# Order of transposes, logits and first loads in a fused attention and expert kernel

## The chip, the cores and the metric

The kernel runs on one core of a Trainium2 chip. The metric is device microseconds of one execution. Before the change the median of three runs is 722.9 us (722.79 to 723.34).

The core's engines are named in the profile as PE (TensorE, matrix products and transposes; PEld is its loading of weights), DVE (VectorE), ACT (ScalarE), POOL (GpSimd) and SP (SyncE, which only issues transfers). Products land in PSUM, eight banks of 512 float32 for each of 128 partitions; another engine has to copy them out.

## The reference

Attention in a sliding window, then a layer of experts of which each token uses one. Everything is float32.

```python
# q, k, v: (8 batches, 8 heads, 576 tokens, 64)
scores = scale * np.matmul(q, k.transpose(0, 1, 3, 2))
mask = (rel >= 0) & (rel < 64)              # a token sees itself and 63 before it
scores = np.where(mask, scores, -1e9)
attn = softmax(scores)
out = np.matmul(attn, v)
x = out.transpose(0, 2, 1, 3).reshape(4608, 512)
logits = x @ w_gate                          # (4608, 8)
expert_idx = np.argmax(logits, axis=1)
gate_w = softmax(logits)[token, expert_idx]
for e in range(8):                           # w1: (8, 512, 1024), w2: (8, 1024, 512)
    h = np.maximum(x[of e] @ w1[e], 0.0)
    y[of e] = h @ w2[e]
return gate_w[:, None] * y
```

## The kernel before, in words

**Two stages.** The attention stage runs from 0 to about 215 us and writes x, already multiplied by its gate, to a table in DRAM (`x_dram`). The expert stage gathers x by expert in tiles of 256 tokens, multiplies it by w1 and w2 (in a form with seven products instead of eight, which is where `left_sums` and `right_sums` belong) and scatters the rows to the output. The order of instructions on every engine is the order in which the code emits them (`manual_schedule`); each engine works through its own list and waits where an operand or a buffer is not ready.

**Units and steps.** The batches are taken two at a time (`bg`, four groups of batches) and the heads two at a time (`g`, four pairs): 16 units. The 1152 tokens of a unit are nine blocks of 128 and are worked on in three steps of three blocks (`ST` = 3, `NST` = 3): `N` = 48 steps in all. A unit's q and k come as eight transfers of 128 KB (`load_qk`), its v as four (`load_v`). The last 64 tokens of every batch, the rests, are loaded once for a group of batches (`load_rests`: two transfers each for q, k and v). GpSimd copies v into a second tile, shifted by a window.

`step(s)` (line 940) is a pipeline by hand, which works on several steps' data at once:

- `scored(s + 1)`: the scores of the next step on TensorE, into banks 0 and 1 (line 627); `masked` (VectorE, line 640) and `softened` (six exps on ScalarE, line 650) follow at once in those engines' lists.
- `weighted(s - 1)`: probabilities times values, into bank 6 (line 673); `divided(s - 1)` on VectorE divides by the sum and writes x (line 687).
- `logit(s - 3)`: the logits of one step, three products into bank 7 (line 710), which gathers them over the four pairs of heads.
- `flipped(s)`: six transposes of the probabilities, one bank for each head (line 658); VectorE copies the first bank out, ScalarE the second (line 660).
- `turned(s + 3)`: the transposes of q and of k for a later step (line 594, four each, one bank each, copied by ScalarE, line 599), or in a unit's third step two transposes of the rests (line 586) in one bank. A step with q and k is called long here and a step with the rests short.
- `x_turned(s - 2)`: three transposes of x (line 698), copied by ScalarE (line 701).
- then the operations that were put down for this step (`todo`).

**The ring of banks.** All these transposes take their banks from one ring of four, `tr_ring` (banks 2 to 5), in the order in which they are emitted. A transposed group can start when the copy that empties the bank's last content is done.

**Routing.** When a group of batches has its logits (`ripe`), `by_tokens` copies them to SBUF and transposes them, one step's worth after the other, and `choose` finds the expert, the gate and the rank of each token, cut into parts that are put down for later steps by `after`. `place` (VectorE) prepares the tables of tokens, `weigh` (GpSimd, some on ScalarE) multiplies x by its gate, `store` sends x to `x_dram`. For the third group of batches `after` ends with `first_tiles` in step 45: two operations of VectorE, 54 small products (line 913), one operation of VectorE that makes the table `perm_e`, and `gather_first`, which gathers the first tile of the expert stage from `x_dram` on GpSimd (line 284). The gather waits for the stores of x.

**The end of the stage.** After step 47 the code emits by hand: the last `weighted`, `turn()` (transposes of the gathered rows, line 305), the last logits and transposes of x among the first products of expert 0 (`tile0`, line 343), and the routing of the last group of batches. The first products use banks 0, 1 and 6.

**The start.** SP issues, in this order: unit 0's q and k, the gate's weights, a row of zeros for `x_dram`, the rests, unit 0's v, unit 1's q and k, unit 1's v, unit 2's q and k. ScalarE's queue carries four transfers of w1 in steps 1, 2, 4 and 5.

Of the kernel before, what the change touches and what calls it, by code (L numbers as in the profile page):

```python
# [11 lines left out]
F32 = mybir.dt.float32  # L12
# [24 lines left out]
def kernel(  # L37
# [10 lines left out]
    nc = tc.nc  # L48
    P = nc.NUM_PARTITIONS
    B, H, S, D = q.shape  # L50
    NT, DM = out.shape
    E = moe_w_gate.shape[1]
# [3 lines left out]
    NG = H // 2  # L56
# [28 lines left out]
    ident = consts.tile([P, P], F32, name="ident")  # L85
# [409 lines left out]
    with tc.manual_schedule(), ExitStack() as held, ExitStack() as brief:  # L495
# [2 lines left out]
        rp = held.enter_context(tc.tile_pool(name="rp", bufs=2))  # L498
        att = brief.enter_context(tc.tile_pool(name="att", bufs=2))
        xp = brief.enter_context(tc.tile_pool(name="xp", bufs=3))  # L500
        sc_ring, tr_ring = cycle((0, 1)), cycle((2, 3, 4, 5))


# [32 lines left out]
        def load_qk(u):  # L536
            bg, g = units[u]
            qks[u] = [qk_m(((u % 3 + 2) % 3 * 2 + n) * 1024, BG, NV, 2, D) for n in range(2)]
            for i in range(BG):
                for t, src in zip(qks[u], (q, k)):  # L540
                    for h in range(2):
                        nc.sync.dma_start(
                            out=t[:, i, :, h, :],
                            in_=src[bg * BG + i, 2 * g + h, 0:SM, :].rearrange("(p j) d -> p j d", j=NV),
                        )

        def load_rests(bg):

            at = 6144 + bg % 2 * 2048
            vr = qk_m(at + 1024, BG, H, D)  # L550
            rests[bg] = [qk_m(at, H, D), qk_m(at + 512, H, D), vr]
            for t, src in zip(rests[bg], (q, k)):
                for i in range(BG):
                    nc.sync.dma_start(
                        out=t[i * D : (i + 1) * D], in_=src[bg * BG + i, :, SM:S, :].rearrange("h p d -> p h d")
                    )
            for i in range(BG):
                nc.sync.dma_start(out=vr[D:P, i], in_=v[bg * BG + i, :, SM:S, :].rearrange("h p d -> p h d"))
# [105 lines left out]
        def weighted(s, pTs):  # L664
            u, c = divmod(s, NST)
            bg, g = units[u]
            va, vb = v_ring[u % NVR]
            px = banks[6](0, 2, ST, VW)
            for m in range(ST):
                for a, (bp, i) in enumerate(blocks_of(c * ST + m)):  # L670
                    vt = va[:, bp, i // 2] if i % 2 or i == 0 else vb[:, bp, i // 2 - 1]
                    for h in range(2):
                        nc.tensor.matmul(  # L673
                            px[a * D : (a + 1) * D, h, m, :], lhsT=pTs[h][:, m, a * D : (a + 1) * D],
                            rhs=vt[:, h, :], start=True, stop=True, skip_group_check=True,
                        )
            return px
# [35 lines left out]
                )  # L713
            return g == NG - 1

        def by_tokens(bg, c):

            if c == 0:
                logits_of[bg] = rp.tile([P, NTB, E], F32, name="logits")
            lgT = rp.tile([ST * GE, P], F32, name="lgT")  # L720
            nc.scalar.copy(out=lgT[:], in_=lgs[bg][:, c, :])
            yield
            tr = banks[next(tr_ring)](0, ST, P)
            nc.tensor.transpose(out=tr[:, 0, 0 : ST * GE], in_=lgT[:], identity=ident[0 : ST * GE, 0 : ST * GE])
            V.tensor_copy(
                out=logits_of[bg][:, c * ST : (c + 1) * ST, :],
                in_=tr[:, 0, 0 : ST * GE].rearrange("p (m e) -> p m e", e=GE)[:, :, 0:E],
            )

        last = B // BG - 1  # L730
# [146 lines left out]
        def after(s, routing, bg):  # L877
# [16 lines left out]
            for m in range(NTB):  # L894
                do(3 + m // 3, partial(place, bg * NTB + m))
                do((2, 2, 3, 3, 4, 4, 4, 5, 5)[m], partial(weigh, bg, m, nc.scalar if m in (2, 6) else G))
                if m % ST == ST - 1:
                    do(3 + m // ST, partial(store, bg, m // ST, G))
            do(6, first_tiles)

        def first_tiles():

# [4 lines left out]
                out=hi_e[:], in0=_inner(key[:], NE * C), in1=_ins(hi_id[:, C + 1 : C + 1 + NE * C], 1, NJE),  # L907
                op=ALU.is_equal,
            )
            slots = banks[next(tr_ring)](0, NE * C)  # L910
            for j in range(NJE):
                for i in range(2):
# [2 lines left out]
                    )  # L915
            V.tensor_scalar(out=perm_e[:], in0=slots, scalar1=-1.0, scalar2=float(NT), op0=ALU.mult, op1=ALU.add)
            gather_first(perm_e[:, 0:C])

        N = NU * NST
        load_qk(0)  # L920
        nc.sync.dma_start(out=wg[:, :, 0:E], in_=moe_w_gate.rearrange("(g p) e -> p g e", p=P))
        nc.sync.dma_start(out=x_dram[NT : NT + 1, :], in_=zrow[:])
        load_rests(0)
        load_v(0)
        load_qk(1)
        load_v(1)
        load_qk(2)

        for g in range(NG):
            step = NST * (g // 2) + g % 2 + 1  # L930
# [9 lines left out]
        def step(s):  # L940
            if 0 <= s + 1 < N:
                prs[s + 1] = softened(*masked(s + 1, scored(s + 1)))
            if 0 <= s - 1 < N:
                px = weighted(s - 1, pTs.pop(s - 1))
            ripe = 0 <= s - 3 < N and logit(s - 3)
            if 0 <= s < N:
                pTs[s] = flipped(prs.pop(s))
            if 0 <= s - 1 < N:
# [8 lines left out]
                    load_qk(u + 3)  # L957
            if s + 3 < N:
                turned(s + 3)
            if 0 <= s - 2 < N:  # L960
                x_turned(s - 2)
            for op in todo.pop(s, ()):
                op()
            if ripe:
                bg, c = (s - 3) // (NG * NST), (s - 3) % NST
                parts = by_tokens(bg, c)
                next(parts)
                todo.setdefault(s + 1, []).append(partial(next, parts, None))
                if c == NST - 1:
                    after(s + 1, choose(bg), bg)  # L970


        for n, s in enumerate((N - 6, N - 3)):
# [174 lines left out]
```

## Time and profile before

| what | value |
|---|---|
| median of the runs | 722.9 us (722.79 to 723.34) |
| the profiled execution | 721.0 us, span 719.3 us, mean granted TensorE clock 0.986 |
| busy over the span | PE 687.2, PEld 606.0, DVE 495.5, ACT 258.6, POOL 350.3 us |
| 0 to 28.2 us (first loads, first steps) | PE 18.8, DVE 10.0, ACT 14.2, POOL 12.6 us busy; clock 0.94 |
| 28.2 to 178.3 us (steps 3 to 40) | PE 149.3, DVE 126.3, ACT 129.9, POOL 84.1 of 150.1 us busy; clock 1.00 |
| 178.3 to 215.5 us (steps 41 to 47 and the first transposes behind) | PE 30.7, DVE 27.2, ACT 22.6, POOL 25.8 of 37.2 us busy; clock 0.91 |
| 215.5 to 719.3 us (experts) | PE 488.5 of 503.8 us busy; clock 0.99 |
| a long step, a short step | 4.07 and 3.42 us from scores to scores |

A line of the timeline gives the start, the length, the engine, the line of the kernel, the operation, out<-in with shapes, the number of instructions merged, and in brackets how long the engine was idle before and what ended that. A product of float32 counts as two instructions of PE, a transpose as one. An idle time matters where the engine is the one that the next work waits for. The granted clock is the share of TensorE's full clock.

### The profile page before, as it was taken

How to read it: one execution, taken by the hardware profiler on the slowest of the kernel's cores; microseconds unless marked ns; L12 is line 12 of the kernel's file. 1: busy time of each engine (PE TensorE's matmuls, PEld its weight loads, DVE VectorE, ACT ScalarE, POOL GpSimd, SP SyncE). 2: the span in 40 equal slices, each digit the busy share in tenths (PEclk: the TensorE clock that was granted, in tenths of full speed). 3: DMA queues.
4: the chain of work that ended last, by engine and by line, in shares of the span. 5: the costliest groups of instructions: out<-in, count | busy, mean ns of one | idle time of the engine just before them, and what ended most of it. 6: DMA issues, size and time to landing. Idle time of an engine off the chain costs nothing. (4 is left out here: it accounts for less than half of the span.)

```text
span 719.3 us, 17940 instructions
## 1 busy us (share of the span) xinstructions
PE 687.2 (96%) x6882; PEld 606.0 (84%) x6882; DVE 495.5 (69%) x1636; ACT 258.6 (36%) x653; POOL 350.3 (49%) x360
## 2 busy tenths in 40 slices
PE   5999999999879999999999999999999999999992
PEld 3788888888769897897999999999899799889992
DVE  3576898898956768676676677568666668756731
ACT  4788888888745012101221111112111122111110
POOL 4223648469573108767451545645266745262001
PEclk9999999999989999999999999999999999999997
DMA  8997789879433364517102620630441810211000
GB/s 158 220 212 176 167 195 236 205 177 248 166 106 117 117 221 171 172 59 282 46 16 84 215 84 31 230 125 15 151 169 59 282 59 6 63 31 61 15 18 29
DMA packets 137293, 93.41 MB, mean 130 GB/s; under 512 B 117008, under 2 KB 117008, under 8 KB 137170
## 3 DMA queue, kind: packets, MB, share of 16 engines
q1 hardware_dynamic: 127858, 62.16, 32.2%
q0 software_dynamic: 8736, 27.53, 11.7%
q10 hardware_dynamic: 576, 2.10, 1.0%
q8 instruction: 74, 1.21, 0.7%
q14 instruction: 49, 0.40, 0.2%
HBM read 72.89 MB, written 20.45 MB: 130 GB/s over the span
## 5 line engine op out<-in xcount | busy, mean ns | idle before, releaser
L314 DVE STREAM_TRANSPOSE v_m<-qk_m 32x256 f32<-32x256 f32 x304 | 132.3, 435 | 9.1 <-DMA qk_m<-x_dram,at_g 2.9
L343 PE MATMUL bank<-qk_m,s 128*128 128x128 f32 x1024 | 122.5, 275 | 0.7 <-DVE qk_m L364 0.7
L343 PEld LDWEIGHTS bank<-qk_m,s 128*128 128x128 f32 x1024 | 118.3, 192 | 0.9 <-issue 0.9
L274 POOL DMA_INDIRECT qk_m<-x_dram,at_g x38 | 41.0, 1079 | 141.5 <-DVE v_m L314 113.1
L650 ACT ACTIVATE pr<-pr,mx 128x128 f32<-128x128 f32 x288 | 89.7, 390 | 33.0 <-DVE mx L640 32.7
L343 PE MATMUL bank<-qk_m,w 128*128 128x128 f32 x768 | 93.9, 275 | 0.6 <-PEq L1076 0.6
L343 PEld LDWEIGHTS bank<-qk_m,w 128*128 128x128 f32 x768 | 90.6, 192 | 4.1 <-issue 3.7
L294 POOL DMA_INDIRECT out_dram<-v_m,at_s x42 | 42.4, 1010 | 87.7 <-DVE v_m L383 85.6
L640 DVE CUSTOM_DVE_ANT_0 pr<-bank,mask 128x128 f32<-128x128 f32 x288 | 64.4, 286 | 27.6 <-PE bank L627 26.3
L383 DVE TENSOR_TENSOR v_m<-bank,v_m 128x256 f32<-128x256 f32 (+1 forms) x95 | 43.8, 480 | 44.7 <-PE bank L387 30.1
L568 POOL COPY v_m<-v_m 64x520 f32<-64x520 f32 x32 | 19.8, 620 | 68.8 <-DMA v_m<-in_v_dram 66.1
L139 POOL TENSOR_TENSOR s<-w 128x1024 f32<-128x1024 f32 x22 | 52.2, 2374 | 0.0
L673 PEld LDWEIGHTS bank<-v_m,pT 128*64 128x64 f32 x1152 | 41.1, 140 | 11.4 <-DVE xs L687 5.2
L673 PE MATMUL bank<-v_m,pT 128*64 128x65 f32 x1152 | 47.8, 231 | 2.5 <-DVE xs L687 2.5
L350 ACT COPY qk_m<-bank 128x512 f32<-128x512 f32 x16 | 9.4, 587 | 108.3 <-PE bank L343 70.0
L387 PE MATMUL bank<-qkT_m,v_m 128*128 128x256 f32 x216 | 48.3, 379 | 0.0
L627 PE MATMUL bank<-qkT_m 64*64 64x128 f32 x1152 | 45.6, 290 | 0.1
L387 PEld LDWEIGHTS bank<-qkT_m,v_m 128*128 128x128 f32 x216 | 41.0, 190 | 5.5
L443 PEld LDWEIGHTS bank<-qk_m,w 128*128 128x128 f32 x320 | 43.9, 190 | 0.9 <-issue 0.7
L443 PE MATMUL bank<-qk_m,w 128*128 128x160 f32 x320 | 44.4, 299 | 0.4 <-ACT qk_m L326 0.4
L594 PE MATMUL bank<-ident,qk_m 128*128 128x128 f32 x256 | 35.7, 283 | 7.7 <-DMA qk_m<-in_q_dram 7.0
L658 PE MATMUL bank<-ident,pr 128*128 128x128 f32 x288 | 43.0, 287 | 0.0
(174 smaller groups left out, 1226.9 us busy)
## 6 DMA issues: line engine op xcount, KB each, us to landing
w<-in_moe_w_dram SPq DMA_DIRECT2D x11, 2048.0 KB, 9.5
qk_m<-in_q_dram SPq DMA_DIRECT2D x72, 128.0 KB, 3.4
qk_m<-in_k_dram SPq DMA_DIRECT2D x72, 128.0 KB, 3.5
v_m<-in_v_dram SPq DMA_DIRECT2D x64, 128.0 KB, 3.9
qk_m<-in_moe_w_dram SPq DMA_DIRECT2D x3, 2048.0 KB, 10.9
x_dram<-xs POOLq DMA_DIRECT2D x6, 512.0 KB, 4.2
x_dram<-xs POOLq DMA_DIRECT2D x3, 768.0 KB, 5.2
w<-in_moe_w_dram ACTq DMA_DIRECT2D x4, 512.0 KB, 4.5
```

The lines of the kernel that those rows point to most:

```text
L139: op()
L294: put = G.indirect_dma_start(out=out[:, :], out_offset=bass.IndirectOffsetOnAxis(ap=at_s[:, c : c + 1], axis=0), in_=ys[c], in_offset=None ...
L314: V.transpose(out=xn[b * QD : (b + 1) * QD, :, :, a * QD : (a + 1) * QD].rearrange("p c g i -> p (c g) i"), in_=rows[a * QD : (a + 1) * QD ...
L343: nc.tensor.matmul(acc[:, f, :], lhsT=a[:, g, f * P : (f + 1) * P], rhs=b[:, g, :], start=(first and f == 0 and g == 0), stop=(g == HG - 1 ...
L383: plus = lambda out, a, b: V.tensor_tensor(out=out, in0=a, in1=b, op=ALU.add)
L387: nc.tensor.matmul(acc, lhsT=a[:, f, :], rhs=b[:, f, :], start=(start and f == 0), stop=(stop and f == HF - 1), skip_group_check=True,)
L443: nc.tensor.matmul(acc[:, i], lhsT=w1[:, g, f * P : (f + 1) * P], rhs=xq[:, g].rearrange("p c s -> p (c s)")[:, 0:HALF], start=(i + g == 0 ...
L627: nc.tensor.matmul(out_, lhsT=qT[rows, t, a * WINDOW : (a + 1) * WINDOW], rhs=rhs, start=True, stop=True, skip_group_check=True,)
L640: V.tensor_tensor_reduce(out=prs[h][:, m, :], in0=scs[h][:, m, :], in1=mask[:, m0 + m, :], scale=-scale, scalar=-2 * MASKED, op0=ALU.add, ...
L650: nc.scalar.activation(out=y, in_=y, func=AF.Exp, scale=-1.0, bias=mx[:, h, m : m + 1])
L658: nc.tensor.transpose(out=tr[:, m, :], in_=prs[h][:, m, :], identity=ident[:])
L673: nc.tensor.matmul(px[a * D : (a + 1) * D, h, m, :], lhsT=pTs[h][:, m, a * D : (a + 1) * D], rhs=vt[:, h, :], start=True, stop=True, skip_ ...
```

## The change

- **x first.** `x_turned(s - 2)` is emitted ahead of `flipped(s)`, where it was behind `turned(s + 3)`. The order of the ring in a step was two of the probabilities, q, k, x; it becomes x, two of the probabilities, q, k.
- **Logits by unit.** The logits of a unit's three steps are emitted together, in the unit's third step, and `by_tokens` takes all three steps of a group of batches at once: one copy, three transposes into one bank, one copy. The end of the stage still uses one step's worth at a time.
- **First table a step later.** `first_tiles` is cut in two: its first VectorE operations stay in step 45, the products, the table and the gather move to step 46.
- **Last values in score banks.** The values of steps 46 and 47 go to banks 0 and 1 instead of 6.
- **First loads.** k of unit 0 and the rests' k of the first batches are issued on ScalarE's queue. On SP the order is unit 0's q, the rests, unit 1's q and k, v of units 0 and 1, the gate's weights, unit 2's q and k, the row of zeros.

```diff
+        lt = brief.enter_context(tc.tile_pool(name="lt", bufs=1))
         sc_ring, tr_ring = cycle((0, 1)), cycle((2, 3, 4, 5))
@@ load_qk
-                for t, src in zip(qks[u], (q, k)):
+                for t, src, queue in zip(qks[u], (q, k), (nc.sync, nc.sync if u else nc.scalar)):
                     for h in range(2):
-                        nc.sync.dma_start(
+                        queue.dma_start(
@@ load_rests
-            for t, src in zip(rests[bg], (q, k)):
+            for t, src, queue in zip(rests[bg], (q, k), (nc.sync, nc.sync if bg else nc.scalar)):
                 for i in range(BG):
-                    nc.sync.dma_start(
+                    queue.dma_start(
@@ weighted
-            px = banks[6](0, 2, ST, VW)
+            px = banks[6 if s < N - 2 else s - N + 2](0, 2, ST, VW)
@@ by_tokens
-        def by_tokens(bg, c):
+        def by_tokens(bg, c, n=1):
...
-            lgT = rp.tile([ST * GE, P], F32, name="lgT")
-            nc.scalar.copy(out=lgT[:], in_=lgs[bg][:, c, :])
+            lgT = (rp if n == 1 else lt).tile([ST * GE, n, P], F32, name=f"lgT{n}")
+            nc.scalar.copy(out=lgT[:], in_=lgs[bg][:, c : c + n, :])
             yield
-            tr = banks[next(tr_ring)](0, ST, P)
-            nc.tensor.transpose(out=tr[:, 0, 0 : ST * GE], in_=lgT[:], identity=ident[0 : ST * GE, 0 : ST * GE])
+            tr = banks[next(tr_ring)](0, n, ST * GE)
+            for i in range(n):
+                nc.tensor.transpose(out=tr[:, i], in_=lgT[:, i], identity=ident[0 : ST * GE, 0 : ST * GE])
             V.tensor_copy(
-                out=logits_of[bg][:, c * ST : (c + 1) * ST, :],
-                in_=tr[:, 0, 0 : ST * GE].rearrange("p (m e) -> p m e", e=GE)[:, :, 0:E],
+                out=logits_of[bg][:, c * ST : (c + n) * ST, :],
+                in_=tr.rearrange("p n me -> p (n me)").rearrange("p (m e) -> p m e", e=GE)[:, :, 0:E],
             )
@@ after
-            do(6, first_tiles)
+            table = first_tiles()
+            do(6, partial(next, table))
+            do(7, partial(next, table))
@@ first_tiles
+            yield
             slots = banks[next(tr_ring)](0, NE * C)
...
             gather_first(perm_e[:, 0:C])
+            yield
@@ first loads
         load_qk(0)
+        load_rests(0)
+        load_qk(1)
+        load_v(0)
+        load_v(1)
         nc.sync.dma_start(out=wg[:, :, 0:E], in_=moe_w_gate.rearrange("(g p) e -> p g e", p=P))
+        load_qk(2)
         nc.sync.dma_start(out=x_dram[NT : NT + 1, :], in_=zrow[:])
-        load_rests(0)
-        load_v(0)
-        load_qk(1)
-        load_v(1)
-        load_qk(2)
@@ step
-            ripe = 0 <= s - 3 < N and logit(s - 3)
+            ripe = 0 <= s - 3 < N and s % NST == NST - 1 and [logit(n) for n in range(s - 5, s - 2)][-1]
+            if 0 <= s - 2 < N:
+                x_turned(s - 2)
             if 0 <= s < N:
                 pTs[s] = flipped(prs.pop(s))
...
             if s + 3 < N:
                 turned(s + 3)
-            if 0 <= s - 2 < N:
-                x_turned(s - 2)
             for op in todo.pop(s, ()):
                 op()
             if ripe:
-                bg, c = (s - 3) // (NG * NST), (s - 3) % NST
-                parts = by_tokens(bg, c)
+                bg = (s - 3) // (NG * NST)
+                parts = by_tokens(bg, 0, NST)
                 next(parts)
                 todo.setdefault(s + 1, []).append(partial(next, parts, None))
-                if c == NST - 1:
-                    after(s + 1, choose(bg), bg)
+                after(s + 1, choose(bg), bg)
```

## The prediction

> **What bounds the kernel now.** I read the page's busy shares first, then windows by stage, then the timeline of one step of the attention stage, then who waits for whom, last the timelines of the head and of the end of that stage. Page, with the clock row:
>
> ```profile
> PE 687.2 (96%) x6882; PEld 606.0 (84%) x6882; DVE 495.5 (69%) x1636; ACT 258.6 (36%) x653; POOL 350.3 (49%) x360
> ...
> PEclk9999999999989999999999999999999999999997
> ```
>
> TensorE is the bound, but the change touches only 0 to 215 us, where the windows show TensorE idle 9.4 us before 28.2, 0.8 in 28.2 to 178.3 (ScalarE 130 and VectorE 126 busy of 150) and 6.5 in 178.3 to 215.5. So there is something to win at both ends, and in the middle only by less matmul work. One long step (four transposes each of q and k), timeline of TensorE; columns are start, length, engine, line:
>
> ```profile
> 102.49 0.89 PE L627 MATMUL bank<-qkT_m 64*64 64x128 f32 x24
> 103.31 0.97 PE L673 MATMUL bank<-v_m,pT 128*64 128x65 f32 x24
> 104.21 0.42 PE L710 MATMUL bank<-xT,wg 128*32 128x128 f32 x6
> 104.56 0.88 PE L658 MATMUL bank<-ident,pr 128*128 128x128 f32 x6
> 105.27 1.04 PE L594 MATMUL bank<-ident,qk_m 128*128 128x128 f32 x8
> 106.14 0.49 PE L698 MATMUL bank<-ident,xs 128*128 128x128 f32 x3
> 106.56 0.89 PE L627 MATMUL bank<-qkT_m 64*64 64x128 f32 x24
> ```
>
> From start to start: scores 0.82, values 0.90, logits 0.35, probabilities' transposes 0.71, q and k 0.87 (0.109 each), x 0.42: 4.07. A short step (rests, two transposes) takes 3.42. The same step on VectorE and ScalarE:
>
> ```profile
> 103.54 0.29 DVE L640 CUSTOM_DVE_ANT_0 pr<-bank,mask 128x128 f32<-128x128 f32 x1 [0.21 <-PE bank L627]
> ...
> 103.87 1.86 ACT L650 ACTIVATE pr<-pr,mx 128x128 f32<-128x128 f32 x6
> ...
> 105.64 0.46 ACT L660 COPY pT<-bank 128x384 f32<-128x384 f32 x1
> ```
>
> Masking begins when the scores are done; the exps begin E after the scores' start (here 1.38) and take 1.77 up to ScalarE's next instruction.
>
> The transposes' banks are a ring of four, so a group waits for the evacuation of the group four places earlier. Before, x is fifth and waits for the step's first probability copy; it shows where VectorE is late:
>
> ```profile
> 186.38 0.55 DVE L660 COPY pT<-bank 128x384 f32<-128x384 f32 x1
> ...
> 186.99 0.55 PE L698 MATMUL bank<-ident,xs 128*128 128x128 f32 x3 [1.42 <-DVE pT L660]
> ```
>
> The copy ends 186.93, TensorE goes on 0.06 later; all such waits are 4.3 us.
>
> **Steps 3 to 40, x moved ahead.** Order of banks now: q, k, after x: x, p0, p1, q, k. k, not x, is now the fifth, and k takes the bank of the same step's x. ScalarE evacuates that x behind the next step's six exps, which it was given first. So k can start at E + 1.77 + 0.48 (x copy, L701) + 0.06, and the next scores start 4 x 0.109 + 0.09 later (x itself: 0.42 = 3 x 0.109 + 0.09): a long step is E + 2.84, with E = 1.38 it is 4.22, although TensorE's work without the logits would be 4.07 - 0.35 = 3.72. The logits taken out of long steps thus go into a wait. The E of the 26 long steps 3, 4, 6, 7, ... 39, 40, read from the timeline, sum to 43.1 and their lengths to 108.5: new lengths 43.1 + 26 x 2.84 = 116.9, +8.4. Where E is above 1.4 (1.8 to 2.7 at steps 16, 21, 24, 28, 31, 33, 40) VectorE is late, from routing and from the place instructions; before, that lateness is hidden behind the rest of the step; after, it is on the path. If the longer steps let VectorE catch up wholly, E is about 1.36 and the sum is +0.7. I take +8.0, near the read E: the step after a lengthened one is less late, but one after a short step is later, because the batched logits there push the first probability copy back by about 0.7 where the step grows by 0.4.
>
> **Logits by unit.** One group of three goes from 0.35 in every step to nine in the short step. A lone group's 0.35 is six passes in three column groups side by side and a drain; two more groups add passes only. Weight loads of 0.025 (0.15 for six) give +0.30; two passes of 0.109 per group give +0.44; two full groups would be +0.70. I take +0.40, nearest the passes, for 13 short steps (5 to 41): +5.2 (3.9 to 9.1). The tokens' transposes (L724) cost 0.09 + 0.14 + 0.09 to 0.15 per group of batches before and three in a row after: nothing, hidden or not. Their copies become one on ScalarE (0.26 x 3 to about 0.48) and one on VectorE (0.18 x 3 to about 0.25); two places, off TensorE's path except through E: within 0.3 for the three groups of batches. The new pool of one buffer is rewritten once in 12 steps; no wait. Each of the three buffers of x is rewritten right behind the batch that read it, which TensorE has passed by the time the copy comes up: nothing.
>
> **The head.** SP issues one 128 KB piece per 0.66 us; TensorE waits for pieces until 20 us:
>
> ```profile
> 18.52 0.63 PE L594 MATMUL bank<-ident,qk_m 128*128 128x128 f32 x4 [1.80 <-DMA qk_m<-in_q_dram]
> ...
> 21.83 1.62 PE L673 MATMUL bank<-v_m,pT 128*64 128x65 f32 x24
> ...
> 25.12 0.89 PE L627 MATMUL bank<-qkT_m 64*64 64x128 f32 x24
> ```
>
> Six pieces (k and its rests) go to ScalarE's queue: 6 x 0.66 = 4.0 us on ScalarE before its table load (1.28, at 0.81 before), together about 6.1, against its first copy at 5.97: 0.1 late. The gate and the zero row move behind: 1.0 us less ahead. Unit 2, ahead of the zero row and behind everything else, is needed at step 3. v moves behind unit 1, so values(0) waits for 24 pieces, 3.15 MB, and behind it on TensorE stand the flips of step 1 and unit 1's second half. Data flows from 2.25 us; at 215 GB/s (busy slices 200 to 220) that is 14.6, 1.15 to land (the first pair, 4.82 less 2.25 less 1.4), and GpSimd's three copies 1.4: 19.4, where values(0) started at 21.83: -2.4. Scores, flips and unit 1 all come earlier than that, TensorE is then waiting for v, and it is warm or not: 21.83 to 25.12 took 3.29, at full clock 0.90 + 0.71 + 0.87 = 2.5. Between -2.4 and -3.2 I take -3.0; bounds 0 (two queues get in each other's way by 2.4) and -4.2 (230 GB/s, warm). By the rows issue was the limit, by little: 0.66 a piece against 0.61 at 215 GB/s. [...] If nothing but the new order counted, values(0) would come at 24 x 0.66 + 3.5 + 1.4 = 20.7, and the head would give -1.1 instead of -3.0.
>
> **The end of the stage.** Before, the table's matmuls stand in TensorE's order before the last scores and wait for VectorE:
>
> ```profile
> 202.01 1.58 PE L913 MATMUL bank<-hi_e,lo 128*128 128x4 bf16 x54 [2.69 <-DVE hi_e L906]
> ...
> 203.52 1.55 PE L627 MATMUL bank<-qkT_m 64*64 64x128 f32 x24
> ...
> 206.12 1.12 POOL L284 DMA_INDIRECT qk_m<-x_dram,perm_e  x1 [3.11 <-DVE mx L640]
> ...
> 209.56 0.97 PE L673 MATMUL bank<-v_m,pT 128*64 128x65 f32 x24 [0.88 <-DVE xs L687]
> ...
> 212.90 0.97 PE L673 MATMUL bank<-v_m,pT 128*64 128x65 f32 x24 [0.88 <-DVE xs L687]
> 213.79 1.09 PE L305 MATMUL bank<-ident,qk_m 128*128 128x128 f32 x8
> ```
>
> After the 2.69 the granted clock is 0.50 over 202 to 207 (scores 1.55 instead of 0.89). A step later the matmuls find their operand (hi_e) ready, and the score banks remove the two waits of 0.88 (the products that use banks 0 and 1 next come after both divisions, and before they waited on bank 6 no less): 2.69 + 2.5 + 1.76 = 7.0 at most. But the first gather at 206.12, with its memset and the second pair moved along on GpSimd, where nothing stands between, is not held by the table (ready 203.9): the last stores of x, issued until 202.5, take about 3.6 to land. GpSimd's chain of weighing sets those, and it starts with ScalarE's weighing in step 42, which moves with E there (3.75). The second gather starts at 208.06 and lands 3.4 later, at 211.5; after, with ScalarE 0.4 later in step 42 and the table ready about 206.8 (exps of step 45 to 202.5, 1 later than before; x and p1 copies to 203.3; values, x and flips 2.0; table 1.3; VectorE 0.2), at about 212.5. Turning gathered rows ends then at 213.0 instead of 214.8. So -1.8, whatever steps 42 to 47 gain or lose; bounds -3.3 (nothing late) and +1.7 (TensorE idle before the gather, and clock 0.5 for one stretch of 3.4 us). Later work keeps its order and is shifted.
>
> **Sum.** -3.0 + 8.0 + 5.2 - 1.8 = +8.4 on the profiled execution's 721.0 (span 719.3): 729.4. The median of the runs, 722.9, stands 1.9 above: 731.3, I say 731.
>
> **Rivals.**
> - *VectorE catches up*: +0.7 in the long steps: 722.9 + 0.7 + 5.2 - 4.8 = 724. For it: VectorE is idle 24 of 150 us; against: its lateness returns in every group of batches.
> - *k isn't held* (the other side): if k's start did not wait for x's copy, long steps become 3.72: 26 of them 96.7 instead of 108.5, or -11.8; total -11.8 + 5.2 - 4.8 = -11.4: 711.5. It decides from a mean long step of 4.16 (26 x 0.016 = 0.4, what the rest leaves): the mean before is 4.17. Against it: the wait at 186.99 shows the ring; for it only that no row shows k itself waiting.
> - *Ends pay nothing*: v lands late (0), clock falls before the gather (+1.7): 722.9 + 13.2 + 1.7 = 738.
>
> **How the numbers follow.** Main case 0.60, 726 to 736 on its own; VectorE catches up 0.18 (721 to 726); k not held 0.09; ends pay nothing 0.13. Leaving out the third case and the top of the last: 720.5 to 738. A measurement can tell about 0.2% (1.4 us): faster 0.09 + 0.05 of the second case, same 0.06, slower 0.80.
>
> **What would show it.** Right: k's transposes idle about 0.5 us in long steps behind ScalarE's x copy, long steps 4.2 or more, short 3.8; values(0) at 19 to 20; no wait at the table, the gather's landing before the turn instead. Wrong: long steps at 3.7; q and k in one run without a gap; logits' nine taking 1.05; a halved clock in the steps.

## The result

The changed kernel takes 735.6 us (median of 4 runs, 735.32 to 738.44) where the kernel before takes 723.1 us on the same chip: a ratio of 1.0171, 95% interval 1.0148 to 1.0194. It is slower by 12.5 us; +8.4 and 731 were forecast. Times are medians over the executions; one execution of the kernel with only the end changed took 1402 us and is not in its ratio. The profiled execution took 735.83 us with a span of 734.1 us, against 721.0 and 719.3 before, which is 14.8 us of span.

The page of the changed kernel first, its busy times and its clock row:

```profile
PE 689.5 (94%) x6882; PEld 608.9 (83%) x6882; DVE 492.6 (67%) x1630; ACT 259.6 (35%) x647; POOL 351.3 (48%) x360
...
PEclk9999999999999999999999999999999999999997
```

TensorE has as many instructions as before and 2.3 us more busy time (689.5 against 687.2), while the span grew by 14.8. So the loss is idle time of TensorE and not work. The page's list of the costliest groups says which idle time (after the second bar: idle time just before the group, and the releaser that ended most of it):

```profile
L595 PE MATMUL bank<-ident,qk_m 128*128 128x128 f32 x256 | 41.6, 292 | 21.6 <-ACT xT L702 14.3
```

L595 holds the transposes of q and k of the long steps. TensorE stands before them for 14.3 us because of one ScalarE copy, that of the transposed x. The timeline of two steps of the changed kernel shows the mechanism (start, length, engine, line, operation, wait in brackets; VectorE's rows are left out):

```profile
105.50 0.82 PE L659 MATMUL bank<-ident,pr 128*128 128x128 f32 x6
...
105.76 1.86 ACT L651 ACTIVATE pr<-pr,mx 128x128 f32<-128x128 f32 x6 [1.98 <-DVE mx L641]
...
106.16 0.60 PE L595 MATMUL bank<-ident,qk_m 128*128 128x128 f32 x4
...
107.53 0.45 ACT L702 COPY xT<-bank 128x384 f32<-128x384 f32 x1
107.89 0.47 ACT L661 COPY pT<-bank 128x384 f32<-128x384 f32 x1
108.04 0.66 PE L595 MATMUL bank<-ident,qk_m 128*128 128x128 f32 x4 [1.28 <-ACT xT L702]
108.63 0.89 PE L628 MATMUL bank<-qkT_m 64*64 64x128 f32 x24
...
112.29 0.66 PE L595 MATMUL bank<-ident,qk_m 128*128 128x128 f32 x4 [0.31 <-ACT xT L702]
```

The transposes of x (L699) start at 105.12 and end by 105.67 (the flips, the transposes of the probabilities, follow at 105.50), but the copy that empties their bank stands in ScalarE's order behind the six exponentials of the next step, and starts at 107.53. q's four transposes run at 106.16, k's four need the bank of x and wait 1.28 us. Four and a quarter microseconds on, the next long step shows the same wait, 0.31 us there because its exponentials were not late.

Stretch by stretch, from the starts of the steps in the two timelines (step s begins with scores(s+1)), and against the prediction's terms:

| stretch | predicted | profiled execution |
|---|---|---|
| up to the start of step 3 | -3.0 | -1.9 |
| 26 long steps, 3 to 40 | +8.0 | +10.4 |
| 13 short steps, 5 to 41 | +5.2 | +5.2 |
| step 42 to the first product of expert 0 | -1.8 | +0.4 |
| after it | 0 | +0.7 |
| sum | +8.4 | +14.8 |

The medians are 12.5 apart and not 14.8, since the median before (723.1) stands 2.1 us above its profiled execution and the median after 0.2 below its own. The table compares one execution with one: executions of one kernel differ by more than a microsecond (the kernel before took 720.6 to 728.2 over 31 of them), so its small terms are uncertain by about as much.

The head of the changed kernel, first the issues of SyncE, then TensorE, then two windows (the stretch, its length, busy times of TensorE, its weight loads, VectorE, ScalarE and GpSimd, granted clock, DMA share, GB/s):

```profile
0.82 2.98 SPq L543 DMA_DIRECT2D qk_m<-in_q_dram  x4
4.22 2.77 SPq L555 DMA_DIRECT2D qk_m<-in_q_dram  x2
...
19.70 0.46 PE L674 MATMUL bank<-v_m,pT 128*64 128x65 f32 x8
20.90 0.73 PE L674 MATMUL bank<-v_m,pT 128*64 128x65 f32 x16 [0.74 <-POOL v_m L573]
...
23.24 0.89 PE L628 MATMUL bank<-qkT_m 64*64 64x128 f32 x24
...
6.00:14.00 8.00, 6.38 (x44) 4.87 (x44) 1.17 (x11) 4.46 (x8) 2.00 (x6) 1.00 1.40 175
14.00:20.00 6.00, 6.00 (x70) 4.94 (x68) 2.08 (x16) 4.57 (x14) 0.34 (x1) 1.00 1.31 217
```

SyncE's pieces of 128 KB follow each other every 0.75 us (2.98 for four) and then every 1.39 (2.77 for two), where it was 0.66 before. An issue itself still takes 0.6 to 0.85 us; the 2.77 for two holds 1.5 us in which SyncE stood, by the profile, until an earlier piece of q had landed. The transfers moved 175 GB/s from 6 to 14 us, with the DMA engines' share at 1.40, and 217 only from 14 to 20. The first values still start at 19.70, 2.1 us earlier than before, but their second part waits for v, and scores(3), with which step 2 begins, come at 23.24, 1.9 us earlier.

The end of the stage, TensorE and GpSimd of the changed kernel:

```profile
201.82 0.66 PE L595 MATMUL bank<-ident,qk_m 128*128 128x128 f32 x4 [2.68 <-ACT xT L702]
...
203.25 1.62 PE L674 MATMUL bank<-v_m,pT 128*64 128x65 f32 x24
...
219.25 1.50 PE L918 MATMUL bank<-hi_e,lo 128*128 128x4 bf16 x54
221.87 1.12 POOL L284 DMA_INDIRECT qk_m<-x_dram,perm_e  x1 [4.61 <-DVE perm_e L921]
...
225.43 0.66 PE L305 MATMUL bank<-ident,qk_m 128*128 128x128 f32 x4 [0.32 <-DMA qk_m<-x_dram,perm_e]
227.31 1.11 PE L305 MATMUL bank<-ident,qk_m 128*128 128x128 f32 x4 [1.22 <-DMA qk_m<-x_dram,perm_e]
229.63 2.34 PE L343 MATMUL bank<-qk_m,w 128*128 128x128 f32 x16
```

The wait of 2.69 us at the table is gone: L918 waits for nothing. Three things take its place. In step 42 ScalarE's exponentials are late, so k waits 2.68 us for the copy of x. Right behind that wait TensorE's clock is halved from 203.1 to 206.5 (values 1.62 us instead of 0.97). And the gather now waits for the table, 2.62 us behind the start of its matmuls. TensorE then waits for the two landings, and its clock drops once more (0.50 from 227.0 to 230.4), so that the second turn takes 1.11 instead of 0.66 and the first product 2.34 instead of 1.95.

### The profile page after: what moved, and what is told of

It is laid out like the page before. It is cut to its first block, busy times and chain, and to the rows that moved or that the text cites. A ratio compares the mean times of both kernels' runs of the same rounds, so it can differ in the third digit from the quotient of the medians.

```text
span 734.1 us, 17901 instructions
## 1 busy us (share of the span) xinstructions
PE 689.5 (94%) x6882; PEld 608.9 (83%) x6882; DVE 492.6 (67%) x1630; ACT 259.6 (35%) x647; POOL 351.3 (48%) x360
## 5 line engine op out<-in xcount | busy, mean ns | idle before, releaser
L595 PE MATMUL bank<-ident,qk_m 128*128 128x128 f32 x256 | 41.6, 292 | 21.6 <-ACT xT L702 14.3
L595 PEld LDWEIGHTS bank<-ident,qk_m 128*128 128x128 f32 x256 | 30.6, 148 | 28.2 <-ACT xT L702 20.6
L661 DVE COPY pT<-bank 128x384 f32<-128x384 f32 x48 | 26.7, 556 | 27.6 <-PE bank L659 23.2
## 6 DMA issues: line engine op xcount, KB each, us to landing
w<-in_moe_w_dram SPq DMA_DIRECT2D x11, 2048.0 KB, 10.3
```

Source lines behind the costliest of these rows:

```text
L595: nc.tensor.transpose(out=tr.rearrange("d a b -> d (a b)").rearrange("d (p j) -> d j p", j=NV)[:, j, :], in_=t[:, c, j].rearrange("p h d - ...
```

## The experiments

The theory was that x ahead of the flips is the whole loss, through k's wait for a copy that stands behind the exponentials, and that the other parts are worth little. The rivals were that the logits by unit or the first loads bring the loss, or that the place of x is innocent and the steps are longer for another reason. Ratios are to the kernel before, run on the same chip.

**x back in its old place, all else of the change kept**

```diff
-            if 0 <= s - 2 < N:
-                x_turned(s - 2)
             if 0 <= s < N:
                 pTs[s] = flipped(prs.pop(s))
...
             if s + 3 < N:
                 turned(s + 3)
+            if 0 <= s - 2 < N:
+                x_turned(s - 2)
```

> The change with only the transposes of x at their old place, behind q and k. Theory (k waits for ScalarE's copy of x behind the exps): the waits at k vanish, a long step becomes 4.07 - 0.35 = 3.72 us, 26 of them 9.1 under the kernel before, short steps stay at 3.85 (+5.2), head -1.9: about 717 us. Rival (what costs is the batch of logits in the short steps and the longer lists of VectorE, x's place matters little): long steps stay above 4.1 and the time at 732 to 736.

Measured: 721.4 us, ratio 0.9966 (0.9944 to 0.9988). The long steps are 3.72 us where nothing else is late, and no k waits for a copy of x. So without the moved x the other three parts together are a small gain, and 14 us of the changed kernel hang on the place of x. They gained less than expected. Scores(3) stand at 25.57, later than before (25.12), because the first values waited for v three times (1.46, 0.93 and 0.72 us) and what followed ran at half the clock (flips 1.54 us instead of 0.87, q and k 1.92 instead of 1.04, scores 1.56 instead of 0.89). Steps 3 to 41 together take 1.0 longer than before: the long steps give 4.4, the short ones take 5.4.

**x ahead alone, on the kernel before**

```diff
             ripe = 0 <= s - 3 < N and logit(s - 3)
+            if 0 <= s - 2 < N:
+                x_turned(s - 2)
...
-            if 0 <= s - 2 < N:
-                x_turned(s - 2)
```

> The kernel before with only the transposes of x moved ahead of the probabilities'. Theory: a long step is again E + 2.87 (E: from the scores' start to the exps'), although it has a group of logits in it, so 4.22 and more; short steps stay at 3.42; together +8 to +11 on 723, 731 to 734 us. Rival (x's place matters little): within 1.5 us of 723.

Measured: 735.7 us, ratio 1.0173 (1.0142 to 1.0204), as slow as the whole change and above the expected 731 to 734. Step 6 of this kernel, ScalarE and TensorE:

```profile
42.57 0.34 ACTq L963 DMA_DIRECT2D w<-in_moe_w_dram  x1
43.02 1.86 ACT L650 ACTIVATE pr<-pr,mx 128x128 f32<-128x128 f32 x6 [2.38 <-DMA qk_m<-in_q_dram]
43.27 0.60 PE L594 MATMUL bank<-ident,qk_m 128*128 128x128 f32 x4
44.78 0.45 ACT L701 COPY xT<-bank 128x384 f32<-128x384 f32 x1
...
45.29 0.66 PE L594 MATMUL bank<-ident,qk_m 128*128 128x128 f32 x4 [1.42 <-ACT xT L701]
```

The same order of events as in the changed kernel. Here E, the time from the start of the scores to the exponentials, is 3.17 (39.85 to 43.02; ScalarE had been idle for 2.38 us: ahead of the exponentials in its list stands the issue of a transfer of w1, which by the profile was held until a load of q landed), and the step takes 6.03 = E + 2.86. Undisturbed long steps take 4.24, again E + 2.86, with the logits still inside: they simply fill a part of k's wait. The 26 long steps are 11.1 us longer, the short steps 1.5. This also shows why the parts don't add: the logits that the change takes out of the long steps free time in which TensorE must wait anyhow.

**Logits by unit alone**

```diff
-            ripe = 0 <= s - 3 < N and logit(s - 3)
+            ripe = 0 <= s - 3 < N and s % NST == NST - 1 and [logit(n) for n in range(s - 5, s - 2)][-1]
...
-                bg, c = (s - 3) // (NG * NST), (s - 3) % NST
-                parts = by_tokens(bg, c)
+                bg = (s - 3) // (NG * NST)
+                parts = by_tokens(bg, 0, NST)
```

> The kernel before with only the logits by unit. Theory: the 0.35 us of a group leaves the 26 long steps (3.72 instead of 4.07, -9.1), the short ones grow by 0.40 (+5.2), nothing takes the place: 719 us. Rival (VectorE or ScalarE, busy 126 and 130 of 150 us, is the next bound close behind TensorE): long steps stay at 4.0 to 4.1 and the time comes to 723 to 728 us.

Measured: 723.0 us, ratio 0.9994 (0.9971 to 1.0016). Long steps are 3.72 and short ones 3.85 where nothing is late, in sum 0.35 less and 0.43 more. Over 26 and 13 steps that would be -3.5. It was given back. In step 9 of this kernel, which starts 0.8 us earlier than before, TensorE runs into the loads:

```profile
54.53 0.63 PE L595 MATMUL bank<-ident,qk_m 128*128 128x128 f32 x4 [1.14 <-DMA qk_m<-in_q_dram]
55.47 0.63 PE L595 MATMUL bank<-ident,qk_m 128*128 128x128 f32 x4 [0.31 <-DMA qk_m<-in_k_dram]
```

and in the steps where routing keeps VectorE busy its copies come late for the next matmuls (step 17 takes 4.79 us instead of 3.58). So the rival had the time right, though the undisturbed long steps are at 3.72 as the theory said: what they give is taken back by waits for loads and for VectorE's copies.

**First loads alone**

```diff
-                for t, src in zip(qks[u], (q, k)):
+                for t, src, queue in zip(qks[u], (q, k), (nc.sync, nc.sync if u else nc.scalar)):
...
         load_qk(0)
-        nc.sync.dma_start(out=wg[:, :, 0:E], in_=moe_w_gate.rearrange("(g p) e -> p g e", p=P))
-        nc.sync.dma_start(out=x_dram[NT : NT + 1, :], in_=zrow[:])
         load_rests(0)
-        load_v(0)
         load_qk(1)
+        load_v(0)
         load_v(1)
+        nc.sync.dma_start(out=wg[:, :, 0:E], in_=moe_w_gate.rearrange("(g p) e -> p g e", p=P))
         load_qk(2)
+        nc.sync.dma_start(out=x_dram[NT : NT + 1, :], in_=zrow[:])
```

> The kernel before with only the first loads changed (k on ScalarE's queue, v behind unit 1, gate and zero row late). Theory: v lands at about 20 where the values of step 0 could start at 17 to 18; TensorE stands 1.5 to 3 us for it, and its clock may be halved for the 3.4 us behind, so the head gives between -1.9 (as in the change's own trace) and +0.5: 721.3 to 723.7 us. Rival (the split of the queues feeds TensorE sooner, as the prediction had it): -3.0, 720 us.

Measured: 723.4 us, ratio 1.0003 (0.9982 to 1.0024). TensorE in the head of this kernel:

```profile
18.83 0.30 PE L673 MATMUL bank<-v_m,pT 128*64 128x65 f32 x2 [1.02 <-DVE mx L640]
20.70 0.70 PE L673 MATMUL bank<-v_m,pT 128*64 128x65 f32 x6 [1.57 <-ACT pr L650]
21.95 1.19 PE L673 MATMUL bank<-v_m,pT 128*64 128x65 f32 x16 [0.55 <-POOL v_m L572]
23.07 1.54 PE L658 MATMUL bank<-ident,pr 128*128 128x128 f32 x6
24.40 1.91 PE L594 MATMUL bank<-ident,qk_m 128*128 128x128 f32 x8
```

The first values begin 3.0 us earlier than before (18.83 against 21.83), come in pieces as v arrives, and end later. (The releasers named at the first two waits are no operands of these matmuls; the experiment with x in its old place has the same three waits, there put down to v's loads and to GpSimd's copy of v.) Behind these waits the flips take 1.54, where the first flips of the same kernel took 0.88, and q and k 1.91 instead of 1.04. The windows of this kernel (columns: the stretch, its length, busy times of TensorE, its weight loads, VectorE, ScalarE and GpSimd, granted clock, DMA share, GB/s) give the clock:

```profile
16.00:18.80 2.80, 1.80 (x34) 1.40 (x32) 2.01 (x16) 2.80 (x10) 0.00 (x0) 1.00 1.00 223
18.80:23.00 4.20, 2.05 (x24) 1.73 (x24) 0.52 (x6) 1.83 (x7) 2.06 (x5) 0.71 0.78 170
23.00:27.40 4.40, 4.40 (x41) 4.00 (x38) 1.38 (x4) 1.65 (x3) 3.62 (x8) 0.50 0.82 178
```

Scores(3) start at 26.25, 1.1 us later than before. The time gained by the second queue is lost to v standing behind unit 1, and to the slow clock that follows the wait (0.50 from 23.0 to 27.4).

**First loads with v still ahead of unit 1**

```diff
         load_qk(0)
         load_rests(0)
-        load_qk(1)
         load_v(0)
+        load_qk(1)
         load_v(1)
```

(the difference to the experiment before this one)

> The same with v of unit 0 ahead of unit 1's q and k; k still on ScalarE's queue. Theory (the order of v is what costs): the values find v, TensorE waits instead at unit 1's transposes, but less than before (gate and zero row gone from ahead, 1.0 us; the first pieces on two queues), the steps' clock is up from the start of step 1: -1.5 to -3 against before, 720 to 721.6 us. Rival (the 16 transfer engines are full, so any order ends alike): within 1 us of head_alone.

Measured: 722.0 us, ratio 0.9989 (0.9979 to 1.0000). The first values start at 20.39 without a wait, and scores(3) at 24.30, 0.8 earlier than before. The order of v makes 1.4 us between the two medians, which the two intervals alone do not tell from nothing, and the second queue with v in its old place gains some 0.8 us, within an interval of 0 to 1.5, less than the 1.5 to 3 expected.

**The end of the stage alone (table a step later, last values in score banks)**

```diff
-            px = banks[6](0, 2, ST, VW)
+            px = banks[6 if s < N - 2 else s - N + 2](0, 2, ST, VW)
...
-            do(6, first_tiles)
+            table = first_tiles()
+            do(6, partial(next, table))
+            do(7, partial(next, table))
```

> The kernel before with only the table a step later and the last values in score banks. Theory: TensorE's wait of 2.7 us and the halved clock behind it go, but the gather starts 0.85 us behind a table that now comes later than the stores, so what is kept is what lies between the last values and the gather's landing: -1.5 to -3, 720 to 721.7 us. Rival (the gather takes it all): within 0.7 us of 723.

Measured: 724.4 us, ratio 1.0027 (1.0008 to 1.0046): the expected gain turned into a small loss. The last scores do start 2.5 us earlier (200.98 against 203.52), although step 42 began 1.4 us later in this execution. But the end waits for the gathered rows, GpSimd and TensorE of this kernel:

```profile
209.06 1.12 POOL L284 DMA_INDIRECT qk_m<-x_dram,perm_e  x1 [4.68 <-issue]
...
212.59 0.66 PE L305 MATMUL bank<-ident,qk_m 128*128 128x128 f32 x4 [2.13 <-DMA qk_m<-x_dram,perm_e]
214.49 0.66 PE L305 MATMUL bank<-ident,qk_m 128*128 128x128 f32 x4 [1.24 <-DMA qk_m<-x_dram,perm_e]
216.16 3.18 PE L343 MATMUL bank<-qk_m,w 128*128 128x128 f32 x16
```

From the start of step 42 the last scores come 3.9 us earlier than before, but the first product only 0.75: most of what was saved in front of the gather is idle time behind it. After that the first product runs 3.18 us at a low clock (0.60 from 216.0 to 219.4) instead of 1.95, and all that follows its start takes 506.4 us instead of 503.7. The timeline names no releaser for this gather, but the trace has the landing of the stores. The last store of x, issued at 203.28, landed at 208.04, 1.02 us before the gather; in the kernel before it was issued at 201.91, landed at 205.11, and the gather came 1.01 behind it. So the stores held it, and the last of them took 4.8 us to land instead of 3.2. The table, whose matmuls started at 205.37, would have let it start at 207.99 (2.62 behind them, as in the changed kernel). Why that store landed late is open.

**The exponentials behind the flips, all of the change kept**

This undoes the suspected cause without moving x: ScalarE gets the copies of x and of the flips first, and then the next step's exponentials.

```diff
             if 0 <= s + 1 < N:
-                prs[s + 1] = softened(*masked(s + 1, scored(s + 1)))
+                hot = masked(s + 1, scored(s + 1))
...
             if 0 <= s < N:
                 pTs[s] = flipped(prs.pop(s))
...
+            if 0 <= s + 1 < N:
+                prs[s + 1] = softened(*hot)
```

> The change with ScalarE's exps of the next step emitted behind the flips of this one, so that its copies of x and of the probabilities come before the exps; x stays ahead. Theory (it is ScalarE's order that holds k, through the bank of x): k's wait goes though the ring's order is the same, long steps fall to 3.7 to 3.9, the time to 712 to 722 us. Rival (the bank ring with x first costs as such, or VectorE's lateness does): long steps stay at 4.2 and more, the time at 732 to 737 us.

Measured: 719.6 us, ratio 0.9956 (0.9938 to 0.9974). x is still ahead, and k no longer waits for its copy. This settles the mechanism: it is not the place of x in TensorE's order that costs, but the place of its copy in ScalarE's. Whether x ahead gains anything by itself is not shown: against x in its old place (721.4, same loads and ends) the two intervals overlap. With the loads of the kernel before in addition:

> The change with the exps behind the flips and the first loads as before. Theory (head neutral to -2, as above): 717 to 721 us, within 2 us of the same kernel with the new loads (719.6). If the new loads gain what the prediction gave them, 3 us slower than that.

Measured: 720.7 us, ratio 0.9966 (0.9943 to 0.9989); the new first loads are within what the two intervals can tell.

**The same with v first, with and without the new ends, and on the kernel before**

With v's first half ahead of unit 1:

> The changed kernel with the exponentials behind the flips, and v's first half ahead of unit 1 of q and k on the first loads. Theory (the first values lose their time to v, which arrives behind unit 1, and to the slow clock after that wait): the wait of some 2.5 us ahead of the first values goes, and what the same move saved on the kernel before, 723.35 - 721.96 = 1.4 us, comes off 719.6: 718.2 (716.5 to 719.5). Rival (the loads are bound by their total, and k of unit 1 waits in v's place): 719.0 to 721.

Measured: 717.6 us (717.44 to 719.26, 6 runs), ratio 0.9925 (0.9905 to 0.9945), the fastest of all. One long step of it, TensorE and ScalarE, shows the order as it should be:

```profile
103.78 0.55 PE L699 MATMUL bank<-ident,xs 128*128 128x128 f32 x3
...
104.17 0.82 PE L659 MATMUL bank<-ident,pr 128*128 128x128 f32 x6
...
104.37 0.48 ACT L702 COPY xT<-bank 128x384 f32<-128x384 f32 x1 [0.17 <-PE bank L699]
...
104.82 1.04 PE L595 MATMUL bank<-ident,qk_m 128*128 128x128 f32 x8
105.08 0.48 ACT L661 COPY pT<-bank 128x384 f32<-128x384 f32 x1 [0.23 <-PE bank L659]
105.45 1.86 ACT L651 ACTIVATE pr<-pr,mx 128x128 f32<-128x128 f32 x6
105.79 0.89 PE L628 MATMUL bank<-qkT_m 64*64 64x128 f32 x24
```

The copy of x follows its transposes by 0.17 us, q and k run as one group of eight, and the exponentials fill ScalarE's time behind. Scores(3) start at 21.83, 3.3 us earlier than before, steps 3 to 41 together are 2.1 longer, and the first product of expert 0 stands at 211.95, 3.6 earlier. So the gain is at the two ends, and the middle is still a small loss. How much of the head's 3.3 is this one execution is not known: with the same loads on the kernel before, scores(3) stood at 24.30. With the ends of the kernel before:

```diff
-            px = banks[6 if s < N - 2 else s - N + 2](0, 2, ST, VW)
+            px = banks[6](0, 2, ST, VW)
...
-            table = first_tiles()
-            do(6, partial(next, table))
-            do(7, partial(next, table))
+            do(6, first_tiles)
```

> The same, with the end of the stage as in the kernel before: the last values in bank 6 and the first table in step 45's place, not a step later. Theory (the later table and the bank changes lost 1.3 us alone, because the gather's landing decides the end): 1.3 us less than with the new ends, 716.9 (715.5 to 718.5). Rival (with faster steps ahead of it the table is no longer late, or is late wherever it stands): the same as with the new ends within 0.5 us, 717.7 to 718.7, or slower by up to 2.5 us, since the last scores start as late as before: up to 720.7.

Measured: 721.9 us, ratio 0.9986 (0.9968 to 1.0003). That is slower than the theory and both rivals allowed (at most 720.7). Here the new ends are worth 4.3 us, although by themselves, on the kernel before, they were a small loss. The end of the fastest kernel shows why:

```profile
202.74 1.50 PE L918 MATMUL bank<-hi_e,lo 128*128 128x4 bf16 x54
...
208.92 0.66 PE L305 MATMUL bank<-ident,qk_m 128*128 128x128 f32 x4 [0.38 <-DMA qk_m<-x_dram,perm_e]
210.63 0.66 PE L305 MATMUL bank<-ident,qk_m 128*128 128x128 f32 x4 [1.05 <-DMA qk_m<-x_dram,perm_e]
...
211.95 1.28 PE L343 MATMUL bank<-qk_m,w 128*128 128x128 f32 x10
```

The waits for the gather are 0.38 and 1.05 here, 2.13 and 1.24 with the ends alone, and the product starts at full clock (1.00 from 187 to 212; 0.128 us a matmul). In the kernel with the old ends TensorE stands 2.99 us before the table's matmuls and its clock is halved from 200.1 to 207.0 (scores 1.56 us instead of 0.89, values 1.62 instead of 0.97); its first product comes at 214.66.

Last, x ahead and the exponentials behind the flips on the kernel before, nothing else:

```diff
             if 0 <= s + 1 < N:
-                prs[s + 1] = softened(*masked(s + 1, scored(s + 1)))
+                hot = masked(s + 1, scored(s + 1))
...
+            if 0 <= s - 2 < N:
+                x_turned(s - 2)
             if 0 <= s < N:
                 pTs[s] = flipped(prs.pop(s))
+            if 0 <= s + 1 < N:
+                prs[s + 1] = softened(*hot)
```

> The kernel before with two moves alone: the transposes of x ahead of the flips, and the exponentials behind the flips in ScalarE's order. Theory (the loss of x ahead is only that the copy of x stands behind the exponentials of the next step, and that k waits for it): all of the +12.5 us goes, the steps are bound by TensorE's own work as before, 722 to 724. Rival (the place of x ahead is worth something by itself once the copy is early): 718 to 721.5. Rival (the exponentials behind the flips hold the flips' copies or the divisions instead, or the flips of the next step wait for them): 725 to 735.

Measured: 732.8 us, ratio 1.0133 (1.0111 to 1.0155): the time of the last rival, and not of the theory, though another copy is held than that rival named. Most long and short steps are back at their 4.07 and 3.42, as the theory said. But in the three groups of steps where the logits' tokens are transposed (13 to 15, 25 to 27, 37 to 39) the same fault turns up with another copy:

```profile
68.24 1.86 ACT L650 ACTIVATE pr<-pr,mx 128x128 f32<-128x128 f32 x6
...
70.94 0.27 ACT L721 COPY lgT<-bank 96x128 f32<-96x128 f32 x1
71.26 0.42 PE L710 MATMUL bank<-xT,wg 128*32 128x128 f32 x6 [0.84 <-ACT lgT L721]
```

The copy of the logits (L721) now stands behind the exponentials and the copies of q and k, and the next logits wait for it, 0.82 to 0.85 us in most of these steps and some 0.5 in the others, 6.5 us in all. These nine steps lose 7.6 of the 10.3 us by which step 46 starts late. With the logits by unit that copy comes once in twelve steps instead of three times. The kernel just above (721.9 us) differs from this one only in the logits and the first loads, and is 10.9 us faster. The first loads account for at most 2.7 of that by scores(3) in the two profiles (21.86 and 24.60), so most of it is the logits by unit, worth nothing alone.

## Why the prediction was right, and where not

- **The time.** 731 was forecast, 735.6 came, and what makes the loss is what the prediction said. Over the profiled executions +8.4 was forecast and +14.8 came: every term but the short steps was too low, so nothing cancelled among them. That the medians miss by 4.6 and not by 6.4 is luck of the executions: the 1.9 us added for the median were not there in the changed kernel.
- **Steps 3 to 40, the mechanism and its formula: right.** k is the fifth group in the ring of four banks, takes the bank of x, and waits for a copy behind the exponentials. The predicted length of a long step was E + 2.84; the trace has E + 2.86 to 2.87, with x alone as well. The term was mis-sized, +8.0 where +10.4 was measured. Against the +8.4 that the E read before give, 1.3 come from step 6, whose E went from 1.33 to 2.61 because the issue of a w1 transfer stood before the exponentials in ScalarE's list until 40.78; 0.7 from the formula (26 times 0.027); and some 0.8 from the three long steps in which the logits' tokens are transposed (E + 3.11) and step 40. In the other 25 steps E fell by 0.7 in sum, where I had taken off 0.4. The x copy, taken as 0.48 behind 1.77 us of exponentials, held.
- **Logits by unit, short steps: right** (+5.2, a short step 3.85 instead of 3.42 in a free run). As the prediction said, what leaves the long steps goes into k's wait; so this term buys nothing, and where k waits the logits are free in the long steps. Taken alone their move is worth 0, since loads and VectorE take back the 3.5 us.
- **The head, -3.0: the step that failed is the rate of the data, and what stands behind the first values.** I let 24 pieces flow at 215 GB/s from 2.25 us on and land by 18.0. They moved at 175 GB/s from 6 to 14 us, and GpSimd could begin to copy v at 19.66. The first values started at 19.70, near the 19.4 of the sum, but only with the part of v that had come; the rest waited 0.74. The term came to -1.9 in the changed kernel. That is one execution and the best of four: with the same first loads scores(3) stood at 23.24, 24.77, 25.57 and 26.25 in four kernels, with those of before at 24.60 to 25.69 in six. Alone the loads came to +1.1 in the profile and to nothing in the median, because v behind unit 1 makes TensorE wait and its clock is halved behind it (0.50 from 23.0 to 27.4); the prediction named a cold TensorE and a late v, and did not take them. The -1.1 that the prediction worked out for the new order alone lies nearer the measured -1.9 and 0 than its own -3.0 does.
- **The end, -1.8: failed, by 2.2.** Two steps of it are wrong. It let steps 42 to 47 gain or lose what they would and counted only the gather's landing, set by the stores of x, ScalarE's weighing in step 42 and a table ready at 206.8. But in step 42, where E is above 3.7 already before, k is held as in the long steps whose sum I ended at step 40: it waits 2.68 us, and the clock is halved behind it (0.50 from 203.1 to 206.5), so steps 42 and 43 take 1.2 us more each and the table comes later. (With x alone ahead k waits 2.33 us in step 42 and step 43 takes 4.25, against 4.24 undisturbed, so most of the second 1.2 belongs to this execution.) On the time scale of before (less the 13.7 us by which step 42 starts late) the first gather was put at 207.2 (a second landing at 212.5, less 3.4 to land and 1.94 between the two gathers) and comes at 208.2, released by the table, which was ready at 207.3 on that scale, 0.85 before it, and not by the stores. The other 1.1 to 1.2 us are the slow clock behind the gather, which I had named as a bound and not taken.
- **After the end, 0: missed by 0.7**, 0.4 of it the first product at a low clock (2.34 us instead of 1.95).
- **Rival "VectorE catches up"** fell: outside step 6, E shrank by 0.7 us in sum, where it needed 7.7. **Rival "k isn't held"** fell in the changed kernel, since 14.3 us of idle time name the copy of x. Its picture of long steps at 3.72 is what appears when the copy comes early, but not its price of -11.8: with the exponentials behind the flips the long steps gave 6.9, because VectorE is next in line: 3.0 us of TensorE's idle time there name its division. **Rival "ends pay nothing"** is the closest in kind: of the predicted -4.8 at both ends -1.5 was left.

## What to carry to other kernels

When a group is moved forward in TensorE's order, move the copy that empties its bank forward in its engine's order too: count for every ring of banks which group reuses which bank, and look what stands before the evacuation in the queue of the engine that makes it, and which other copy the move puts back (here that of the logits). A matmul taken out of a step pays only if the step was bound by matmul; look first at who is next (loads, VectorE, a copy). Measure the parts of a change beside the others too: here two that gained nothing alone, the logits by unit and the later table, pay once the copies are in order.

## What the runs showed of the hardware

- TensorE's granted clock, by the clock records of the kernel before and of the changed one up to 230 us: it was halved from 20.15 to 23.56 and from 201.05 to 207.88 in the kernel before, and from 203.13 to 206.54 and from 227.02 to 230.43 in the changed one, each time for 3.41 us or twice that. In the 3.41 us ahead of these four TensorE was idle for 2.36, 1.74, 2.10 and 1.54 us. In step 42 of the changed kernel 2.10 of the 2.68 us of k's wait fell into the 3.41 us before 203.13, and the next 3.41 us ran at half the clock (values 1.62 instead of 0.97, flips 1.33 instead of 0.82); ahead of the second turn of the gathered rows the idle time was 1.54, and that turn took 1.11 instead of 0.66. Not every wait was followed by a lower clock: behind the 1.42 us at 186.99 in the kernel before it stayed at 1.00, and so it did from 187 to 212 in the fastest kernel, with its waits of 0.38 and 1.05.
- While ScalarE issues too, up to 6.3 us, SyncE's issue of a piece of 128 KB takes 0.6 to 0.85 us, where it took 0.5 to 0.7 alone; and the pieces land hardly faster for the second queue: from 6 to 14 us 175 GB/s in the changed kernel, 166 before.
- The first indirect gather on GpSimd starts 2.62 us behind the start of the table's 54 matmuls, of which the matmuls take 1.50, in four kernels alike (the changed one, and three with the exponentials behind the flips); in the changed kernel that is 0.85 us behind the end of VectorE's write of the table. In the kernel before and in the one with only the end changed it starts 1.01 and 1.02 us behind the landing of the last store of x (205.11 and 208.04).
